# One blank product of 512 columns at the kernel's start becomes sixteen of 64 by 64 columns

## The chip, the core and the metric

The kernel runs on one core of a Trainium2 chip. Five engines work side by side, each from its own instruction stream: TensorE (PE, matrix products; its weight loads are listed as PEld), VectorE (DVE), ScalarE (ACT), GpSimd (POOL) and SyncE (SP), which here issues the DMA transfers. The metric is the time of one execution on the device in microseconds, the median of several runs. Durations below come from one execution that the hardware profiler recorded.

## What is computed

The reference has two stages. The first is a linear recurrence over time (a "retention") for 4 batches and 8 heads, 768 steps, head size 64; the second is a two-layer network with an ELU on the 3072 tokens that come out.

```python
for t in range(S):
    state = gamma * state + einsum('bhd,bhe->bhde', k[:, :, t], v[:, :, t])
    y[:, :, t] = scale * einsum('bhd,bhde->bhe', q[:, :, t], state)
x = y.transpose(0, 2, 1, 3).reshape(B * S, H * D)      # 3072 x 512
h = x @ w_in                                           # 512 x 2048
g = where(h > 0, h, exp(min(h, 0)) - 1)
out = g @ w_out                                        # 2048 x 512
```

All of it is in f32.

## The kernel before

The recurrence is done in chunks of 128 steps, each in two halves of 64. For a chunk the kernel forms scores of k with q inside each half (`score_products`, L290), masks them on DVE (`mask_pair`, L312, or `scores`, L300), scales v (`scale_v`, L259), forms the state contributions k times v (`state_products`, L320), sums the states (`state_sum`, L331), and multiplies masked scores and states with v and q (`outputs`, L349: L364 for the first kind, L390 for the second). All these products are 64 by 64 with 64 columns; a chunk has many of them in a row, and four of them use four different quarters of the PE array. The rest of this text calls such a run a burst.

The tokens are handled in six blocks of 512 (`tb`). For each, the two-layer network follows the retention, with products that are combined by Strassen's scheme, in the later blocks twice nested (`strassen`, `first_twice`, `second_twice`; L834 is the product of the innermost level, 128 by 128 with 128 columns). The weights arrive as 64-bit numbers and are decoded at the start by ACT and DVE (`prepare`, L140, with L155 and L157; `decode`, L167, with L178 to L187). Small combined weights are written to DRAM and read back through a ring of tiles (`fetch_small`, L676).

The order of the instructions on every engine is the order in which the code emits them; nothing reorders them afterwards. An engine takes its instructions in that order and waits on semaphores for what the others deliver. The first loads are chained: a one-element copy on POOL (`hold`, L114, L117) waits for a transfer to land, and only then is the next one issued by SP.

The start of the program, around the change, emits on PE, in this order: two blank products (L984, through `unread`, whose product is L982), the scores of chunk 0 (L986, product L295), a blank product of 256 columns (L989), the state products of chunk 0 (L991, product L326), the first products of the outputs (L364), a blank product of 512 columns (L998), the scores of chunk 1 (L999), and so on. A blank product multiplies a tile of zeros (`blank`, set by DVE at L200) by itself into the PSUM tile `warm`, which nobody reads before it is written again.

On the other engines, behind these: DVE masks the scores (L316), scales v (L269), adds up states (L338) and decodes the first piece of the weights; ACT fills the decay table (L238), copies the first state (L336) and then prepares the weights (L155, L157).

An f32 product is two passes on PE, and each pass has a weight load of its own: a call of `nc.tensor.matmul` becomes four PE instructions.

Of the kernel before, what the change touches and what calls it, by code (L numbers as in the profile page):

```python
# [17 lines left out]
def kernel(  # L18
# [32 lines left out]
    nc = tc.nc  # L51
# [3 lines left out]
    B, H, S, D, DM, DFF = dims  # L55
    NTOK = B * S
    C = P
    TB = 512
# [140 lines left out]
    blank = hpool.tile([P, TB], FP32, name="blank", tag="h")  # L199
# [370 lines left out]
    def bank(x):  # L570
        return ps_f.tile([P, 2, TH], FP32, name="p" + x, tag=x, bufs=2 if x == "a" else 1)
# [406 lines left out]
    warm = bank("a").rearrange("p a b -> p (a b)")  # L978

    def unread(count, n):  # L980
        for _ in range(count):
            nc.tensor.matmul(warm[:, 0:n], lhsT=blank[:, 0:P], rhs=blank[:, 0:n], start=True, stop=True, skip_group_check=True)  # L982

    unread(2, TB)  # L984
    sc = [ps_r.tile([P, 2, HP, D], FP32, name="sc", tag="r") for _ in range(2)]
    score_products(sc, 0, 0, 0)  # L986
    mask_pair(sc, 0)
# [285 lines left out]
```

## Time and profile before

| What | Value |
|---|---|
| median of 4 runs | 646.56 us (646.29 to 648.25) |
| the profiled execution | 648.25 us, its span 646.5 us |
| granted PE clock, mean over the span | 0.997 |
| PE, first 1.45 us | idle, until DVE has zeroed `blank` |
| PE busy, 1.45 to 5.05 us | 3.60 of 3.60 us |
| PE busy, 5.05 to 10.72 us | 3.55 of 5.67 us |
| PE busy, 40 to 80 us | 40.00 of 40.00 us |

"Span" is the time from the first instruction to the last; what lies around it belongs to the start and end of an execution. A row of the timeline has the start in us from the span's start, the length in us, the engine, the line, the operation, the tiles (output<-inputs), the shapes, and how often it is repeated; in brackets the idle time of the engine before it and what ended it. "issue" means that nothing in the profile shows what the engine waited for. A busy PE is not PE at its peak, since products overlap.

### The profile page before, as it was taken

Reading aid. Unit: us, or ns where it says so; the run is one execution under the profiler, and the core shown is the slowest. Engines: PE = TensorE matmul, PEld = TensorE weight load, DVE = VectorE, ACT = ScalarE, POOL = GpSimd, SP = SyncE. Lnnn points to the kernel's source line nnn. Section 1 sums busy time; section 2 is a strip of 40 time slices with the busy share of each in tenths; the row PEclk is TensorE's granted clock in tenths of the full one; section 3 lists DMA queues with packets and bytes.
Section 4 is the critical chain, followed back from the end, with each engine's and each line's share of the span. In section 5 each row is a group of like instructions: output and inputs, shape, how many; then the busy total and the mean of one; then the engine's idle time right before and its main releaser. Section 6 shows DMA issues by size and latency. Waiting matters only on the chain.

```text
span 646.5 us, 15903 instructions
## 1 busy us (share of the span) xinstructions
PE 635.6 (98%) x6526; PEld 543.9 (84%) x6526; DVE 499.0 (77%) x893; ACT 241.0 (37%) x465; POOL 39.8 (6%) x42
## 2 busy tenths in 40 slices
PE   7999999999999899999999999999999999999998
PEld 4774445458889899989999988999988999988998
DVE  5889699898979576489867488868569958557976
ACT  5577631204452112556111465211465311356311
POOL 1001100000450000100000010000020000000000
PEclk9999999999999899999999999999999999999999
DMA  8749778999488689801789820788840688710694
GB/s 304 285 144 379 257 228 223 324 267 271 154 254 281 180 263 302 303 21 44 248 277 284 294 113 11 216 273 290 280 189 3 190 261 264 231 52 1 212 309 165
DMA packets 85209, 139.72 MB, mean 216 GB/s; under 512 B 6672, under 2 KB 38800, under 8 KB 82832
## 3 DMA queue, kind: packets, MB, share of 16 engines
q1 hardware_dynamic: 85136, 138.70, 66.4%
q8 instruction: 52, 0.85, 0.5%
q14 instruction: 21, 0.17, 0.1%
HBM read 114.56 MB, written 24.12 MB: 215 GB/s over the span
## 4 chain that ended last, share of the span: by engine, by line
PE 70%; DVE 7%; DMA 2%; SPq 1%; POOL 1%; issue 1%; ACT 1%; POOLq 0%; DVEq 0%
PE pa L834 20%; PE pa L795 10%; PE pd L834 9%; PE pb L834 5%; PE pa L749 4%; PE pb L795 4%; PE qa L795 3%; PE pd L749 2%; PE qd L795 2%; PE pd L795 2%; POOL wi L700 1%; PE y L364 1%; PE y L390 1%; PE sc L295 1%; PE kv L326 1%
## 5 line engine op out<-in xcount | busy, mean ns | idle before, releaser
L842 ACT COPY ms<-pa 128x128 f32<-128x128 f32 x104 | 27.5, 265 | 147.9 <-PE pa L834 146.4
L834 PE MATMUL pa<-ts,wq 128*128 128x128 f32 x560 | 74.1, 275 | 0.3 <-ACT ms L842 0.3
L834 PE MATMUL pd<-ts,wq 128*128 128x128 f32 x552 | 73.2, 275 | 0.0
L834 PEld LDWEIGHTS pa<-ts,wq 128*128 128x128 f32 x560 | 68.5, 192 | 0.8 <-ACT ms L842 0.5
L834 PEld LDWEIGHTS pd<-ts,wq 128*128 128x128 f32 x552 | 67.1, 192 | 0.3 <-DVE res L846 0.2
L834 PE MATMUL pa<-gC,wq 128*128 128x128 f32 x480 | 65.2, 279 | 0.0
L445 ACT ACTIVATE r<-r 128x512 f32<-128x512 f32 x96 | 60.5, 630 | 3.0
L834 PEld LDWEIGHTS pa<-gC,wq 128*128 128x128 f32 x480 | 59.7, 194 | 1.4
L444 ACT ACTIVATE r<-gC 128x512 f32<-128x512 f32 x64 | 39.9, 624 | 33.2 <-DVE gC L803 33.2
L846 DVE TENSOR_TENSOR res<-pd,ms 128x128 f32<-128x128 f32 x68 | 19.5, 287 | 37.3 <-PE pd L834 36.1
L448 DVE SCALAR_TENSOR_TENSOR gC<-r,gC 128x512 f32<-128x512 f32 x64 | 45.3, 739 | 0.7 <-ACT r L445 0.7
L269 POOL TENSOR_TENSOR kvn<-kvn,vf 128x512 f32<-128x512 f32 x21 | 25.1, 1201 | 329.8 <-DMA kvn<-in_qkv_dram 325.5
L711 DVE TENSOR_TENSOR ts<-gC,ts 128x512 f32<-128x512 f32 x60 | 41.3, 688 | 1.0
L711 DVE TENSOR_TENSOR ts<-gC 128x512 f32<-128x512 f32 x60 | 41.0, 684 | 0.0
L834 PE MATMUL pb<-gC,wq 128*128 128x128 f32 x240 | 32.8, 277 | 0.1
L491 PE MATMUL pa<-gC,w_s 128*128 128x512 f32 x64 | 30.6, 600 | 0.0
L867 ACT COPY res<-pa 128x128 f32<-128x128 f32 x34 | 9.0, 266 | 57.5 <-PE pa L834 56.0
L834 PEld LDWEIGHTS pb<-gC,wq 128*128 128x128 f32 x240 | 29.5, 192 | 0.8 <-DVE gC L448 0.8
L803 DVE TENSOR_TENSOR gC<-qa,gC 128x512 f32<-128x512 f32 x8 | 5.5, 692 | 25.1 <-PE qa L795 18.3
L575 ACT COPY m<-pa 128x512 f32<-128x512 f32 x24 | 13.9, 580 | 24.5 <-PE pa L795 13.2
L795 PE MATMUL pa<-xt,w_s 128*128 128x256 f32 x96 | 23.0, 382 | 0.0
L795 PE MATMUL pa<-xt,w_b 128*128 128x256 f32 x96 | 23.0, 382 | 0.0
(226 smaller groups left out, 1239.0 us busy)
## 6 DMA issues: line engine op xcount, KB each, us to landing
wq<-scratch_dram SPq DMA_DIRECT2D x277, 256.0 KB, 4.4
wraw<-in_w_dram SPq DMA_DIRECT2D x16, 1024.0 KB, 6.9
qk<-in_qkv_dram SPq DMA_DIRECT2D x24, 512.0 KB, 6.4
kvn<-in_qkv_dram SPq DMA_DIRECT2D x24, 512.0 KB, 7.2
scratch_dram<-w_s SPq DMA_DIRECT2D x8, 512.0 KB, 5.0
scratch_dram<-so SPq DMA_DIRECT2D x8, 512.0 KB, 5.0
out_dram<-res SPq DMA_DIRECT2D x14, 256.0 KB, 4.2
scratch_dram<-gT SPq DMA_DIRECT2D x12, 256.0 KB, 4.2
```

Source lines behind the costliest of these rows:

```text
L269: eng.tensor_tensor(out=kv[:, 1], in0=kv[:, 1], in1=vf[:, i].unsqueeze(2).to_broadcast([C, H, D]), op=ALU.mult)
L444: nc.scalar.activation(e, h, AF.Relu, scale=-1.0)
L445: nc.scalar.activation(e, e, AF.Exp, scale=-1.0)
L448: nc.vector.scalar_tensor_tensor(g, e, -1.0, h, ALU.add, ALU.max)
L491: nc.tensor.matmul(ops[d], lhsT=wo[:, row, (d if row else d ^ 2) * P :][:, 0:P], rhs=g_plain[row * NF + f], start=(n == 0 and row == 0), s ...
L575: nc.scalar.copy(m, ps)
L711: sub = lambda o, x, y: nc.vector.tensor_tensor(out=o, in0=x, in1=y, op=ALU.subtract)
L749: nc.tensor.matmul(ps[:, f, :], lhsT=lhs[f], rhs=xs[j][k], start=(begin and f == 0), stop=True, skip_group_check=True,)
L795: nc.tensor.matmul(ps[:, fi, :], lhsT=w[:, fi, j2, :], rhs=x[:, j2, :], start=(j in (1, 7) and fi == 0 and j2 == 0), stop=(j2 == 1), skip_ ...
L834: nc.tensor.matmul(ps, lhsT=w[:, f, :], rhs=ts[j][k][:, f, :], start=(begin and f == 0), stop=(f == 3), skip_group_check=True,)
L842: nc.scalar.copy(m, ps)
L846: nc.vector.tensor_tensor(out=o, in0=x, in1=y, op=ALU.add)
```

## The change

The two blank products at the start become one of 512 columns and sixteen with 64 weight columns and 64 moving columns. All sixteen read the same part of `blank` over all 128 partitions and write the same 64 by 64 corner of `warm`. Nothing else in the kernel differs, and the other blank products stay as they were.

```diff
-    unread(2, TB)
+    unread(1, TB)
+    for _ in range(16):
+        nc.tensor.matmul(warm[0:D, 0:D], lhsT=blank[:, 0:D], rhs=blank[:, 0:D], start=True, stop=True, skip_group_check=True)
     sc = [ps_r.tile([P, 2, HP, D], FP32, name="sc", tag="r") for _ in range(2)]
     score_products(sc, 0, 0, 0)
     mask_pair(sc, 0)
```

TB is 512 and D is 64. The changed kernel has two more lines, so lines behind L984 carry numbers higher by 2; the new product stands at L986. On PE one 512-column product gives way to sixteen small ones; the other four engines have the same instructions in the same order.

## The prediction

> **What bounds the kernel now.** First the page's busy table, where one engine stands out:
>
> ```profile
> PE 635.6 (98%) x6526; PEld 543.9 (84%) x6526; DVE 499.0 (77%) x893; ACT 241.0 (37%) x465; POOL 39.8 (6%) x42
> q8 instruction: 52, 0.85, 0.5%
> ```
>
> TensorE is in work for 98% of the span, and the chain of waits gives it 70%. What PE loses is lost at the end, unless PE would have waited there anyway. The change stands in the first 5 us, so I read the front second, in the timeline:
>
> ```profile
> 1.45 3.65 PE L982 MATMUL pa<-blank 128*128 128x512 f32 x4 [1.45 <-DVE blank L200]
> 5.05 0.34 PE L295 MATMUL sc<-qk 64*64 64x64 f32 x8
> ...
> 7.99 0.37 ACT L336 COPY kvn<-kv 128x256 f32<-128x256 f32 x1 [0.50 <-issue]
> 8.91 0.67 ACT L155 ACTIVATE w_a<-wraw 128x512 uint32<-128x512 uint32 x1 [0.55 <-DMA wraw<-in_w_dram]
> ...
> 10.36 0.43 DVE L178 TENSOR_SCALAR wraw<-wraw 128x512 f32<-128x512 f32 x1 [1.54 <-ACT wraw L157]
> 10.82 0.43 DVE L181 TENSOR_SCALAR wraw<-wraw 128x512 uint32<-128x512 uint32 x1
> 11.46 0.76 DVE L316 TENSOR_TENSOR qk<-sc,cmask 128x256 f32<-128x256 f32 x2 [0.21 <-PE sc L295]
> ```
>
> Two blank products are four passes[...]. The front waits for DMA: sc at 5.05 for qk (landed about 5.04), L155 for the weights, the second sc at 10.72 for the next qk (1.29 idle). These are slack for a late PE.
>
> Third, PE's idle times. From 31 us to the end of the work only one is over 0.35 us, and it has no data as its releaser:
>
> ```profile
> 216.73 0.38 PE L390 MATMUL y<-qk,kvn 64*64 64x64 f32 x11
> 218.92 0.34 PE L390 MATMUL y<-qk,kvn 64*64 64x64 f32 x7 [1.81 <-issue]
> ```
>
> The chain of waits holds these 1.81 us ("issue"). I read them as PE waiting for code. Queue q8 has 52 packets of 16,384 bytes; PE has 6526 products, 6526 loads and 261 other records, 13,313 in all, and 52 x 256 = 13,312: a packet for 256 PE instructions (64 bytes each). Number 15 starts at 216.58, takes 0.92, and PE goes on 1.42 us after it has landed. The next product is PE record 4033 (records counted in order of start), so blocks begin at records 193 + 256k. Of the other fetches none lands less than 1.50 us before its block's first record runs (the one landing at 314.91, needed at 316.40), and none of them stalls: a fetch seems usable about 1.42 us after landing.
>
> **Part 1: the front.** Removed: one 512-column product, two passes. Added: sixteen products 64 by 64, 32 passes and 32 loads, all on the same rows and columns of the array. No DMA, no other engine, no wait is added; they write the same tile. Single rows of the trace show the old passes starting at 2.46, 3.32 and 4.17: 0.853 each, twice the 0.429 of the 512-column passes of L491 later (starts at 96.12, 96.55, 96.98). The fourth takes 0.93 instead of 1.06: the clock rises at about 4.85, where the trace's clock record begins (the 1.00 before it is only the page's default). A pass of 64 columns is an eighth: 0.107 slow, 0.053 fast. The one product left ends its stream at 3.32; by 4.85 there is room for 14.3 small passes, the other 17.7 take 0.94 us, to 5.79. So **sc starts 0.74 us late**. What follows: ACT L336 8.36 + 0.74 = 9.10 at its end, so L155 loses its idle 0.55 and is 0.19 late; L178 and L181 are 0.19 late, and L316 had 0.21 idle before it. The second sc still waits for its DMA, as PE's idle 1.29 covers 0.74. The chunk loads are held by the copies of L117, which wait for DMAs, not for PE. Cost taken: **0.00**. If each pass is 5% longer (L834's 128-column passes: 1.06 less one record of 0.275 is 0.112 each for seven, against 0.107), the delay is 0.83 and 0.07 leaks. Without cover the whole 0.74 would be paid.
>
> [...] The row: L834's eight passes, each with its own load of 192 ns on the same rows, follow each other every 0.112 us; the loads hide.[...] The row decides: 0.00.
>
> **Part 2: what moves.** 4 PE instructions go, 64 come: everything after sits 60 instructions later in the stream, so the blocks begin at old records 133 + 256k.[...] In the old trace, by how many records a burst begins after 193 + 256k, its fetch starts after the burst's start: -11: 1.12 us; -9: 1.16; -2: 1.02; +28: 0.71; +52: 0.51. That is 0.010 us a record. At +82 and +112 the fetch came 5.9 and 6.1 us ahead of the burst. Number 15 (+77, 1.02 instead of 0.26) is an outlier. The bursts concerned:
>
> ```profile
> 207.06 2.08 PE L326 MATMUL kv<-kvn 64*64 64x64 f32 x112
> ...
> 233.52 1.16 PE L364 MATMUL y<-qk,kvn 64*64 64x64 f32 x64
> 234.50 0.65 PE L390 MATMUL y<-qk,kvn 64*64 64x64 f32 x32
> ```
>
> All positions grow by 60; usable = start + about 0.95 (the packet) + 1.42; "needed" is the old time of the new boundary record:
> - Number 15: +137, fetched ahead. The 1.81 us go. Next late is data only, since the records before it have no long wait: **-1.81**.
> - Number 14: +49, starts 207.60, usable 209.96, needed 208.63: **+1.33**.
> - Number 17: +51, starts 234.04, usable 236.42, needed 235.74: **+0.68**.
> - Number 35 (burst at 428.11): +58, usable 430.86, needed 430.78: **+0.08**.
> - Number 44 (burst at 528.52): +88. Ahead of the burst, as at +82: 0; held as at +77: usable 530.96, needed 529.75: 1.21. I take 0, the nearer row.
> - The rest start well ahead (their fetches preceded the bursts before, and now are asked for still earlier): 0.
>
> These are estimates; no shifted stream is in the trace. From below, each new stall can be 0 (sum -1.81); from above numbers 14 and 17 may be as late as number 15 was, 0.76 each, and 44 may stall: 0.28 + 1.52 + 1.21 = +3.0. **Sum taken: +0.28.**
>
> [...]
>
> **Clock.** After the old stall the granted clock was half:
>
> ```profile
> 219.00:220.00 1.00, 1.00 (x13) 0.94 0.76 289
> 220.00:221.00 1.00, 1.00 (x7) 0.50 0.08 31
> ```
>
> (Columns: length, PE busy, clock, DMA share, GB/s.) The clock record puts it at 219.89 to 223.30, 3.41 us, worth 1.71. The profiled execution was 648.25 (span 646.5, 1.75 around it), the other three 646.29 to 646.58: 1.7 less. I take it that they had no such dip; so the median needs no correction, and the profiled execution should fall to 648.25 - 1.71 + 0.28 = 646.8.
>
> **Rivals.**
> - A, the forecast: front hidden, one stall against two smaller. 646.56 + 0.28 = **646.8**; own range 645.3 to 647.85. Chance 0.53.
> - B: the old stall goes and fetches 14 and 17 come early enough: 644.75; if the unprofiled runs had the dip too, 643.0. For it: only one fetch in 52 stalls now. Against: two bursts take the very positions that were tight. 0.16.
> - C, slower: the new stall near 208.6 lowers the clock for a window: 0.28 + 1.71 = 648.55. It decides from a gap between 1.18 (at 9.43, no dip seen) and 1.81 (dip); the estimate 1.33 lies inside. Late fetches (up to +3.0, 649.6) end on the same side. Against: 1.33 is nearer the harmless gap. 0.22.
> - D, slower:[...] the front is over 0.76 late. If the clock stays low, the blanks end at 3.32 + 3.41 = 6.73, 1.7 late with sc; less 0.76, and with sc's own slow passes (0.47), 1.4 at L316: 648.2 with the exchange. Against: DMA waits at 21.70 (qk) and 22.93 (kvn, ACT idle 4.56) would absorb much. 0.09.
>
> Within 0.2% (1.29 us, what a measurement here can tell from none): 645.27 to 647.85. Faster is B, 0.16; slower is C and D, 0.31; same 0.53. The range 644.6 to 648.8 leaves out B with the dip and the worst of C and D.
>
> **What would show it.** L986: 32 passes at about 0.107 then 0.053, ending near 5.8; L155 near 9.1, second L295 still at 10.72 behind DMA. No "issue" gap at 217; gaps in L326 near 208.6 and behind L390 near 236, in front of records 60 earlier than 193 + 256k. I am wrong if L986 runs at over 0.12 a fast pass, if PE at 40 us is late, or if "issue" gaps stand elsewhere.

## The result and the profile after

The changed kernel takes **649.25 us** (median of 43 runs, 646.58 to 653.59) against 646.57 for the kernel before (64 runs): a ratio of **1.0042, 95% interval 1.0032 to 1.0052**, or 2.7 us slower. The ratios here are not quotients of the two medians shown, so they can differ a little from them (most for c204 below, 1.0025 where the medians give 1.0038). The profiled execution took 650.89 us, its span 649.0 (before: 648.25 and 646.5).

The page of the kernel after: the busy table and the code queue.

```profile
PE 637.0 (98%) x6556; PEld 546.0 (84%) x6556; DVE 499.3 (77%) x893; ACT 240.8 (37%) x465; POOL 40.4 (6%) x42
q8 instruction: 52, 0.85, 0.5%
```

The sixteen small products stand as 32 passes and 32 loads, two of each to a call. There are 30 passes and 30 loads more, and PE is busy 1.4 us longer. The span grew by 2.5, so over 1 us is idle time. The front of the kernel after, in the timeline (start, length, engine, line, operation, tiles, shapes, count, idle time before):

```profile
1.45 2.08 PE L982 MATMUL pa<-blank 128*128 128x512 f32 x2 [1.45 <-DVE blank L200]
3.46 3.66 PE L986 MATMUL pa<-blank 128*64 128x64 f32 x32
7.05 0.69 PE L295 MATMUL sc<-qk 64*64 64x64 f32 x32
...
9.98 0.37 ACT L336 COPY kvn<-kv 128x256 f32<-128x256 f32 x1 [2.49 <-POOL wraw L117]
10.25 0.68 ACT L155 ACTIVATE w_a<-wraw 128x512 uint32<-128x512 uint32 x1
...
11.35 0.56 PEld L295 LDWEIGHTS sc<-qk 64*64 64x64 f32 x32 [0.76 <-issue]
```

All 32 small passes ran at half speed, 0.107 us apart, an eighth of the 0.853 of a slow 512-column pass; the clock record begins at 6.97. The first scores come 2.00 late, L155 1.34 late, the second scores 0.63 late. Yet the front is not where the time went: a product of L625 that starts at 148.35 before starts at 147.54 after.

The bursts, in the timelines of the kernel after:

```profile
207.44 1.84 PE L326 MATMUL kv<-kvn 64*64 64x64 f32 x103
211.07 0.50 PE L326 MATMUL kv<-kvn 64*64 64x64 f32 x9 [1.78 <-issue]
...
219.57 1.16 PE L364 MATMUL y<-qk,kvn 64*64 64x64 f32 x64
220.56 0.23 PE L390 MATMUL y<-qk,carry 64*64 64x64 f32 x2
...
235.39 0.94 PE L834 MATMUL pa<-gC,wq 128*128 128x128 f32 x6
237.48 0.38 PE L834 MATMUL pa<-gC,wq 128*128 128x128 f32 x2 [1.15 <-issue]
...
432.29 0.50 PE L834 MATMUL pb<-gC,wq 128*128 128x128 f32 x3
433.44 0.82 PE L834 MATMUL pb<-gC,wq 128*128 128x128 f32 x5 [0.65 <-issue]
```

The 1.81 us in L390 are gone; in their place stand 1.78 in L326, 1.15 behind the burst at 233.8 and 0.65 behind that at 429.7. The products after them are PE records 3777, 4545 and 9153 (counted from 0): 193 + 256k, the places of the forecast, at three of its four bursts. I read them as waits for code from the packets of queue q8 ("instruction"): PE goes on 1.33, 1.52 and 1.47 us after packets 14, 17 and 35 have landed. The same holds for all 31 gaps at block ends in the fourteen traces of this text (1.21 to 1.53 us), and in none of them did a block begin sooner after its packet than 1.21 us. Behind the gap before record 3777 the clock drops, as it did behind the old one (windows of the kernel after: length, PE busy, clock, DMA share, GB/s):

```profile
209.00:210.00 1.00, 0.29 (x14) 1.00 0.72 225
210.00:211.00 1.00, 0.00 (x0) 1.00 0.50 186
211.00:212.00 1.00, 0.93 (x12) 0.88 0.04 16
212.00:213.00 1.00, 1.00 (x7) 0.50 0.00 0
```

The half-clock window lasts from 211.76 to 215.18, 3.41 us like the old one from 219.89, so the two cancel between these two traces.

Lateness of equal products in the two traces, read along the program, adds up to the 2.5: -0.81 at 148; +0.39 at 190 (the transfer from wi to scratch_dram, which PE waits for there, took 5.99 instead of 4.12); +0.31 at 224, behind old and new stall and both clock windows; +1.63 at 238, behind the 1.15; +2.54 at 434, behind the 0.65. From there on nothing is added. The last two steps, 1.32 and 0.91, are larger than the gaps in them, since idle time counts from the end of the last product (0.275 us long) and the next one would have started 0.112 us after that one's start: by this estimate (0.275 - 0.112) a gap understates its stall by about 0.2 us.

### The profile page after: what moved, and what is told of

Its sections match the earlier page's. It is cut to its first block, busy times and chain, and to the rows that moved or that the text cites. A ratio compares the mean times of both kernels' runs of the same rounds, so it can differ in the third digit from the quotient of the medians.

```text
span 649.0 us, 15963 instructions
## 1 busy us (share of the span) xinstructions
PE 637.0 (98%) x6556; PEld 546.0 (84%) x6556; DVE 499.3 (77%) x893; ACT 240.8 (37%) x465; POOL 40.4 (6%) x42
## 4 chain that ended last, share of the span: by engine, by line
PE 90%; DVE 5%; issue 2%; POOL 1%; DMA 1%; ACT 1%; SPq 0%; POOLq 0%; DVEq 0%
PE pa L834 20%; PE pa L795 10%; PE pd L834 9%; PE hp L477 6%; PE pb L834 5%; PE pa L749 4%; PE pa L491 4%; PE pb L795 4%; PE qa L795 3%; PE pd L749 2%; PE qd L795 2%; PE pd L795 2%; PE pd L491 2%; PE pb L491 2%; PE kv L326 2%; PE sc L295 2%
## 5 line engine op out<-in xcount | busy, mean ns | idle before, releaser
L834 PE MATMUL pa<-ts,wq 128*128 128x128 f32 x560 | 74.1, 275 | 0.3 <-ACT ms L842 0.3
L834 PE MATMUL pd<-ts,wq 128*128 128x128 f32 x552 | 73.1, 275 | 0.0
L834 PEld LDWEIGHTS pa<-ts,wq 128*128 128x128 f32 x560 | 68.5, 192 | 0.8 <-ACT ms L842 0.5
L834 PE MATMUL pa<-gC,wq 128*128 128x128 f32 x480 | 65.8, 280 | 2.1 <-issue 1.2
L834 PEld LDWEIGHTS pd<-ts,wq 128*128 128x128 f32 x552 | 67.1, 192 | 0.3 <-DVE res L846 0.2
L834 PEld LDWEIGHTS pa<-gC,wq 128*128 128x128 f32 x480 | 59.9, 194 | 3.9 <-issue 2.6
L834 PE MATMUL pb<-gC,wq 128*128 128x128 f32 x240 | 33.9, 282 | 0.7 <-issue 0.7
L834 PEld LDWEIGHTS pb<-gC,wq 128*128 128x128 f32 x240 | 30.4, 197 | 1.7 <-DVE gC L448 0.9
L846 DVE TENSOR_TENSOR res<-pb,ms 128x128 f32<-128x128 f32 x36 | 10.3, 287 | 17.8 <-PE pb L834 17.8
```

The lines of the kernel that those rows point to most:

```text
L834: nc.tensor.matmul(ps, lhsT=w[:, f, :], rhs=ts[j][k][:, f, :], start=(begin and f == 0), stop=(f == 3), skip_group_check=True,)
L846: nc.vector.tensor_tensor(out=o, in0=x, in1=y, op=ALU.add)
```

## Experiments

Two theories. **Code**: the 60 PE instructions move the ends of the code blocks into bursts, and the time is the stalls there. **Front**: the late first scores, or the late clock, cost the time. A third was added for the second group: the mere number of instructions or of small products.

**Count and lateness apart.** Four kernels, beside the kernel before (646.51 us in this group, 75 runs; 22 of each other kernel).

r1_count_only, the count of the change with passes half as long:

```diff
-    unread(2, TB)
+    unread(1, TB)
+    for _ in range(16):
+        nc.tensor.matmul(warm[0:32, 0:32], lhsT=blank[:, 0:32], rhs=blank[:, 0:32], start=True, stop=True, skip_group_check=True)
```

> Sixteen products of 32 by 32 columns in place of the sixteen of 64 by 64: the same 60 PE instructions more, but the small passes stream as many columns in all as the product they replace, so the front should end near 5 us as before. Code theory (the 60 instructions move the ends of the code blocks into bursts): the change's time, about 1.8 to 2.7 us over before, with issue gaps before records 3777 (1.5 to 1.8 us), 4545 (1.0 to 1.3) and 9153 (0.1 to 0.7), none before 4033. Front theory (the late first scores and the late clock cost the time): no more than 0.5 us over before.

r2_late_only, late with the count of before:

```diff
-    unread(2, TB)
+    unread(3, TB)
...
     scale_v(0)
-    unread(1, TH)
```

> Three blank products of 512 columns in front and the one of 256 columns behind the first scores left out: exactly as many PE instructions as before, but the first scores come about 1.5 to 2 us late, as in the change. Code theory: time of before within 0.5 us, with the one issue gap of about 1.8 us before record 4033, since no block boundary moves. Front theory: 1.5 to 2.7 us over before.

r3_count12:

```diff
-    unread(2, TB)
+    unread(1, TB)
+    unread(4, P)
```

> One blank product of 512 columns and four of 128 in front: as many columns as before, 12 PE instructions more. Code theory: the burst at 215.6 us now begins 89 records behind a block boundary[...], so the 1.81 us gap goes; the burst at 528.5 us comes to stand at 40 and may lose 0 to 0.8; 0.8 to 1.8 us faster than before. Front theory: no change within 0.5 us.

r4_late_count12:

```diff
-    unread(2, TB)
+    unread(3, TB)
+    unread(2, TH)
```

> Three blank products of 512 columns and two of 256 in front: 12 PE instructions more than before, as in the one with four of 128, and twice the columns, so the first scores come 2 to 3.4 us late. Code theory: as the one with four of 128, 0.8 to 1.8 us faster than before. Front theory: 2 us or more slower than before.

| Kernel | PE instructions added | first scores at | time, us | ratio (95%) | full-clock span, us (runs) | from 190 us on, us | issue gaps at block ends in its trace, us before record |
|---|---|---|---|---|---|---|---|
| before | 0 | 5.05 | 646.51 | | 644.25 (44) | 451.83 | 1.81 before 4033 |
| r1_count_only | 60 | 5.30 | 649.04 | 1.0036 (1.0024 to 1.0049) | 646.70 (12) | 453.53 | 2.33 before 3777, 0.86 before 4545 |
| r2_late_only | 0 | 6.25 | 646.55 | 1.0005 (0.9991 to 1.0019) | 644.55 (14) | 452.24 | 1.53 before 4033, 0.36 before 6337 |
| r3_count12 | 12 | 5.16 | 648.18 | 1.0023 (1.0010 to 1.0036) | 646.10 (17) | 452.20 | 0.44 before 3777, 1.03 before 4033, 0.06 before 6337 |
| r4_late_count12 | 12 | 6.53 | 648.15 | 1.0021 (1.0008 to 1.0035) | 646.30 (19) | 452.65 | 0.16 before 3777, 1.58 before 4033, 0.22 before 11457 |

"Full-clock span" is the median span of the runs whose mean granted clock was 1.0, so it is free of half-clock windows. "From 190 us on" is the time in the trace from the first L834 product at about 190 us, where PE comes from a wait for a transfer, to PE's last product, less 1.71 us (half of 3.41) where a half-clock window lies in it; the kernel with the change has 454.08.

The rows pair by count, not by lateness: with 60 more instructions and the scores nearly in time, the time of the change; with the scores 1.2 us late and no instruction more, the time of before. That is the front theory's end as to late scores, up to the 1.2 us tested (1.5 to 2 were expected; the change had 2.00, but was ahead again by 148 us). What stands for the code theory is a line in each trace. In r1_count_only's timeline:

```profile
208.29 1.62 PE L326 MATMUL kv<-kvn 64*64 64x64 f32 x91
212.24 0.71 PE L326 MATMUL kv<-kvn 64*64 64x64 f32 x9 [2.33 <-issue]
```

and in r2_late_only's:

```profile
217.21 0.38 PE L390 MATMUL y<-qk,kvn 64*64 64x64 f32 x11
219.13 0.34 PE L390 MATMUL y<-qk,kvn 64*64 64x64 f32 x7 [1.53 <-issue]
```

The late clock alone is not shown harmless by r1, since its trace has the clock rise at 7.56. In single traces the time does not follow that moment: the clock rose at 4.38 in r4_late_count12, which is slow, and at 5.55 in r2_late_only, which is not. For the untraced runs the moment is not on record.

The code theory's own number for r3 and r4 was wrong: they were to be 0.8 to 1.8 faster and are 1.7 slower. The gap before record 4033 did not go at 12 instructions more, and up to two smaller ones opened. No single distance behind the block end decides: with the burst 89 records behind it, the fetch started 0.18 us after the burst in r3, and 0.21 after another burst in c100 below; at 88 records in the trace after it started 3.26 us ahead of the burst.

**One whole block, and other shifts.** In the second group, kernels with nothing but products of 32 by 32 columns in front (c100: one of 512 columns as well); before took 646.67 us here (67 runs).

```diff
-    unread(2, TB)
+    for _ in range(66):
+        nc.tensor.matmul(warm[0:32, 0:32], lhsT=blank[:, 0:32], rhs=blank[:, 0:32], start=True, stop=True, skip_group_check=True)
```

That is c256. c204 has 53 such products and c228 has 59; c100 has `unread(1, TB)` and 26 of them.

> Sixty-six products of 32 by 32 columns in place of both blank products of 512: 256 PE instructions more than before, one whole block. Code theory, with blocks of 256 instructions: every block ends at the same place of the program as before, so time of before within 0.6 us, and the issue gap stands at the same products (now record 4289, still 193 + 256k), no gap in the products of L326 near 208. If it is the mere number of instructions or of small products that costs: more than the change, over 2.7 us slower than before.

> Fifty-three products of 32 by 32 columns in place of both blank products of 512: 204 PE instructions more, the same as 52 fewer as to the block ends. Code theory: the burst at 215.6 us begins 25 records behind a block end instead of 77, so its gap shrinks to 0 to 0.5 us; the scores at 198.6 us come to 74 and may stall up to 2 us. Between 1.8 us faster and 0.5 us slower than before. Mere number: over 2 us slower.

> Fifty-nine products of 32 by 32 columns in place of both blank products of 512: 228 PE instructions more, the same as 28 fewer as to the block ends. Code theory: the burst at 215.6 us begins 49 records behind a block end, gap about 1.0 to 1.3; the scores at 198.6 us at 98, gap 0 to 2; from 0.8 faster to 1.5 slower than before. Mere number: over 2 us slower.

> One blank product of 512 columns and twenty-six of 32 by 32: 100 PE instructions more. Code theory: the bursts at 207.1, 233.5 and 327.7 us begin 89, 91 and 52 records behind a block end; gaps of about 1 to 2 us at each, 3 to 5 in all against 1.8 before: 1.5 to 3.5 us slower than before. Mere number: between the change with 60 more and that with 204 more, 2 to 4 us slower, so this run alone does not part the two; its gaps do.

| Kernel | added | time, us | ratio (95%) | full-clock span, us (runs) | from 190 us on, us | issue gaps at block ends in its trace, us before record |
|---|---|---|---|---|---|---|
| before | 0 | 646.67 | | 644.55 (46 of 67) | 451.83 | 1.81 before 4033 |
| c100 | 100 | 648.02 | 1.0019 (1.0002 to 1.0035) | 645.95 (10 of 14) | 452.36 | 1.03 before 3777, 0.94 before 6849 |
| c204 | 204 | 649.12 | 1.0025 (1.0008 to 1.0042) | 642.50 (3 of 22) | 451.50 | 1.45 before 705, 0.45 before 1217, 1.30 before 11201 |
| c228 | 228 | 649.76 | 1.0042 (1.0024 to 1.0059) | 643.90 (3 of 22) | 451.39 | 3.70 before 705, 1.23 before 8897 |
| c256 | 256 | 647.36 | 1.0017 (1.0003 to 1.0031) | 645.25 (14 of 22) | 451.70 | 3.20 before 705, 1.26 before 4289, 0.20 before 11713 |

The mere number falls by c256: with 256 more the kernel is 0.7 us slower, with 60 more it was 2.5 to 2.7. (c204 and c228 by themselves came out where that theory put them, over 2 us slower.) c256 is the control for the block: its late gap stands at the same products as before, one block further in the count, none stands in L326, and from 190 us on it takes 451.70 us, within the 451.08 to 452.24 of the four traces with no shift (before, its two further traces below, and r2):

```profile
219.82 0.38 PE L390 MATMUL y<-qk,kvn 64*64 64x64 f32 x11
221.46 0.34 PE L390 MATMUL y<-qk,kvn 64*64 64x64 f32 x7 [1.26 <-issue]
```

Its 0.7 is slightly outside the 0.6 that was expected (its trace comes to the 190 us point 2.8 us late, from the stall before record 705 and the half clock behind it), and c204 and c228 missed their ranges, for a reason I had not foreseen: with over 200 instructions more ahead of the first scores, block ends fall into the bursts of the front. c204's timeline:

```profile
16.59 0.51 PE L326 MATMUL kv<-kvn 64*64 64x64 f32 x11
18.55 0.33 PE L326 MATMUL kv<-kvn 64*64 64x64 f32 x4 [1.45 <-issue]
```

The traces of c228 and c256 hold a half-clock window of 6.83 us from about 18.05 behind that early stall. Among the untraced runs 18 of 22 of c204 and 19 of 22 of c228 had a mean clock of 0.997 or less. So their medians do not measure the later shift. Where neither the front nor the clock counts they are no slower than before: from 190 us on 451.50 and 451.39, and in the three full-clock runs of each spans 2.05 and 0.65 us shorter. Three runs are few, and a run without a half-clock window may also have had the smaller stalls. c204's gap at the burst of 215 us is gone, as expected. c100 had two of the three gaps named, the one behind 233.5 us was missing, and it lies just under its range (1.35 us slower).

**How far one gap varies.** Two more traces each of the kernel before and of r3_count12, unchanged.

> The kernel before once more, for a second trace. Code theory: an issue gap before record 4033 and nowhere else over 0.4 us, of another size than 1.81 if the fetch's delay varies (1.0 to 2.0); a half-clock window of 3.41 us or none.

> As the other look at the kernel before; the two together show how far one gap varies.

> The kernel with four blank products of 128 columns (12 PE instructions more) once more. It was 1.6 us slower than before although its first trace held gaps of only 1.5 us in all. If the gaps vary from run to run: gaps before records 3777, 4033 and perhaps 11457 of 2.5 to 4 us in all. If something else costs: gaps of 1.5 us again, and PE late by over 1 us somewhere else.

> As the other look at the kernel with 12 PE instructions more.

Single executions of 646.39 and 646.69 us for before, 649.29 and 647.80 for 12 more. Before: 0.99 and 1.53 us before record 4033, and in the first of the two also 0.86 before record 449, in the front. With 12 more: 1.99 and 1.55 before 4033, 0.50 and 0.90 before 11457, none before 3777. In the timeline of the first of the two with 12 more:

```profile
218.31 0.32 PE L390 MATMUL y<-qk,kvn 64*64 64x64 f32 x5
220.62 0.45 PE L390 MATMUL y<-qk,kvn 64*64 64x64 f32 x13 [1.99 <-issue]
```

So the same stall runs from 0.99 to 1.81 in four traces of an unmoved stream, and from 1.03 to 1.99 in four with 12 more. All issue gaps at block ends sum to 1.53, 1.96, 2.48 and 2.45 in the four traces with 12 more, on average 2.1, against 1.81, 1.89, 1.85 and 1.53 in the four of before and r2, on average 1.8. As gaps that is 0.3 us of the 1.7 by which r3 and r4 are slower, but gaps understate stalls, and those of before are fewer. From 190 us on the four traces with 12 more take 452.72 us on average, against 451.74 in the four with no shift: 1.0 longer. Up to there they are 0.4 later (190.50 against 190.12); in all four L834 waits for a transfer there (0.73 to 1.32 us; under 0.15 in the other four), and why is open, as is the last 0.3. Traces are of profiled executions, and the untraced runs may stall differently.

By its median, no version tried beats the kernel before.

## Why the prediction was wrong

**What bounds the kernel: right.** PE still has 98%, and its idle "issue" time is what moved the end.

**The front's delay: its size was wrong, its cost right.** The step "by 4.85 there is room for 14.3 small passes, the other 17.7 take 0.94 us" took the moment at which the clock rises as fixed. It isn't: with the first product always at about 1.45, it rose at moments from 4.38 to 7.56 in the thirteen traces that have a clock record, and at 4.39, 4.82 and 4.85 in three of one kernel, before. In the trace after it rose at 6.97, when the last of the 32 small passes had started. So scores were 2.00 late, not 0.74, and L155 1.34; the 0.74 could only have come true by chance. What sets the moment of the rise is not shown. What the clock records show is the distance of the changes: before has a rise at 4.85, a fall at 219.89 and a rise at 223.30, after has them at 6.97, 211.76 and 215.18. From the first rise to the fall are 215.04 and 204.80 us, 63 and 60 times 3.4133, and 3.413 from the fall to the next rise; in all thirteen records the changes are whole multiples of 3.4133 us apart. The cost of 0.00 held all the same: r2_late_only, 1.2 us late, has the time of before, and the trace after is ahead of before at 148 us. The later waits on transfers absorb more than the 0.76 that I had counted as slack. That loads on the same rows hide held too: 0.107 us a pass with a load each, no more than an eighth of the 0.853 of a 512-column pass.

**The exchange of stalls: places right, sizes wrong. This is the step that failed.** Stalls at block ends were exchanged, as forecast, and the places were right in the trace after (numbers 14, 17, 35; 44 none, as taken; 35 none in r1). Sizes, with the two traces that have 60 more instructions (after, r1):

| Stall | predicted | measured |
|---|---|---|
| number 15 goes | -1.81 | gone; it was 0.99 to 1.81 in four traces with no shift, mean 1.47 |
| number 14 | +1.33 | 1.78, 2.33 |
| number 17 | +0.68 | 1.15, 0.86 |
| number 35 | +0.08 | 0.65, none |
| sum | +0.28 | mean of the two 3.39, less 1.47: +1.9 |

With the smaller stalls of those four traces (0.86 and 0.36, at other block ends) the difference is 3.39 - 1.77 = 1.6; as lateness from 190 us on it is 453.81 - 451.74 = 2.1. Two terms were mis-sized. The start of the fetch was taken from a line of "0.010 us a record", 0.52 to 0.54 us behind the start of the bursts of numbers 14 and 17 and 0.45 for 35; it was 1.33, 1.25 and 1.28 in the trace after, and in r1, at the same places in the count, 1.77 and 1.03 behind and 0.84 ahead of the burst. Number 15, set aside as an outlier at 1.02, was the better guide. The trace of before also had three bursts that speak against the line and were left out of it: at +24 (382.87 us), +54 (483.28) and +57 (388.55) the fetch started 5.0, 6.9 and 3.3 us ahead of the burst. What sets the start of a fetch is not shown by any run. The lag from landing to use, 1.42 in the trace of before, held: 1.33, 1.52 and 1.47 in the trace after. And the old stall was credited at the 1.81 of a single trace, which is its upper end. The bound "from above" named just this lateness, +0.76 for each, but the sum was taken from the line.

**The clock: half-clock windows are in the runs of both kernels.** "I take it that they had no such dip": whether those three runs had one is not on record. But among the 75 runs of before in the first group, 44 had a mean clock of 1.0 (median span 644.25 us) and 27 one of 0.997 (645.80), which is what one half-clock window gives (half of 3.41 in 646 is 0.0026). So over a third of before's runs have one somewhere; of its three traces one has it behind the old stall, one at 18.04 us and one not at all. With 60 more instructions the full-clock runs of r1 have a median span of 646.70, 2.45 more than before's in the same group, and those of the changed kernel 646.45 (20 of 44): most of the 2.7 is there without any dip. At 0.997 or less were 23 of 44 with the change, 29 of 75 before; those shares, read across groups, can add a few tenths to a median, not the whole. Rival C, the dip near 208.6, shows in both traces with the shift, and is not the main cause.

Nor does the length of a gap decide on a dip, as rival C had it (its harmless gap of 1.18 is, besides, 1.29 us of idle time in the lines shown). A gap of 1.99 us in look_12_1 (12 instructions more), longer than the 1.81, left the clock at 1.00 (length, PE busy, clock, DMA share, GB/s):

```profile
219.00:220.00 1.00, 0.00 (x0) 1.00 0.60 172
220.00:221.00 1.00, 0.38 (x13) 1.00 0.87 322
221.00:222.00 1.00, 1.00 (x13) 1.00 0.31 119
```

Nor is a busy time shown that decides. With each trace cut into stretches of 3.4133 us from its first rise, PE was busy for 1.60, 1.63, 1.08, 1.15 and 1.45 us in the stretch ahead of the dip in before, after, r1, c228 and c256, and for 2.15 ahead of that in look_before_1; behind stretches with 1.83 (r4), 1.88 (r2 and look_before_2), 2.00 (look_12_1) and 2.12 us (before, 8.26 to 11.67) the clock stayed full.

**Rival D**: the front was over 0.76 late, as it said, and it cost nothing that can be measured. Nor did small products by themselves keep the clock low: in c228 and c256 only products of 32 columns ran before it rose, at 4.41 and 4.38. **Rival B**: only number 15 went. The measured time lies 2.45 above the forecast and 0.45 above the end of the range, and a sum that was 1.3 to 1.8 too small is the larger part of it; the rest is in part the dips, in part open.

## What to carry to other kernels

Here 60 PE instructions more at about 3.5 us moved the block ends by 60 records, and the gaps at block ends (1.78, 1.15 and 0.65 us) stood at 209 to 433 us, far behind the edit. After an edit that adds or removes PE instructions in another kernel bound by PE, look for "issue" gaps far from it as well, number PE's records, and see whether the gaps lie a whole block (here 256) apart. Test a small edit against a control with the same number of instructions and another content, and against one with the same content and the number restored. Take the size of such a stall from several traces. Don't take the moment of the clock's rise as fixed (4.38 to 7.56 us here), and compare the runs at full clock apart from the others.

## What the runs showed of the hardware

- Queue q8 ("instruction") moved 52 packets of 16,384 bytes, before and after. Stalls of up to 3.70 us (c228) stood at steps of 256 PE instructions (records 193 + 256k) in every trace, mostly where a block ended in or just behind a run of small products, and PE went on 1.21 to 1.53 us after the packet had landed.
- The same stall in the same program varied by 0.8 us from one execution to the next (0.99 to 1.81), with 12 instructions more by 1.0 (1.03 to 1.99).
- The changes of the clock were whole multiples of 3.4133 us apart in all thirteen traces with a clock record (215.04 is 63 of them in before, 204.80 is 60 in after). In the stretch of this length ahead of a fall PE was busy for 1.08 (r1_count_only) to 2.15 us (look_before_1); behind stretches with 1.83 (r4_late_count12) to 2.12 us (before) a full clock stayed. So these traces show no busy time that parts the two.
- A half-clock window of 3.41 us costs about 1.55 us by the two groups of before's runs (645.80 less 644.25); those runs may differ in their stalls too.
- The clock rose 2.93 us after the first product in r4_late_count12 (at 4.38, first product at 1.45), 3.40 after it in before (4.85) and 5.51 in after (6.97).
